# Reordering the first block of a convolution-and-MLP kernel: VectorE work pinned, halo from DRAM, plain output products, and last stores over three queues

## The chip, the cores and the metric

The kernel runs on one core of one Trainium2 chip. The metric is the time of one execution on the device, in microseconds (us). All timed runs told here were in the fast one of the two states in which executions of one program fall. Engine names in profile lines: PE is TensorE, PEld its weight loads, DVE VectorE, ACT ScalarE, POOL GpSimd, SP SyncE; a "q" after a name is the engine's own sequencer, where it issues DMAs. A record is one entry of the trace; each product of this kernel shows as two records.

## The reference

Each of 32,768 tokens has 192 channels. A causal convolution of seven taps, softmax-normalised per head, is followed by a two-layer MLP with silu:

```
w   = softmax(weight, axis=-1)                  # 8 heads, 7 taps
h   = causal_conv(x, w)                         # x: (8, 4096, 192); a sequence starts with 6 zeros
a   = h @ w_in                                  # 192 -> 2048
out = (a * sigmoid(a)) @ w_out                  # 2048 -> 192
```

## The kernel before

The tokens are worked off in 32 blocks of 1024. A block is turned by VectorE (transposes), convolved on VectorE (three channel groups of one first tap and six further taps; a half of the block also needs the six tokens before it, its halo), copied to both partition halves by DMA ("spread", tile `dup`), and multiplied on TensorE by `w_in` and `w_out` in four chunks j = 0..3. Blocks 1 to 31 use a form with fewer products and more additions. Block 0 has extra work, because all weights have to be rounded on VectorE first (`rounded`), with two steps of each rounding on ScalarE:

```
def rounded(dst, key):                     # cut: ten steps, here the order that matters
    nc.vector.tensor_single_scalar(ex, hi, ...)
    nc.vector.tensor_single_scalar(st, lo, ...)
    nc.vector.tensor_scalar(ex, ex, ...)
    nc.scalar.sign(st, st)                               # ScalarE
    nc.scalar.activation(ex, ex, AF.Copy, ...)           # ScalarE
    nc.vector.tensor_scalar(mh, hi, ...)
    ...                                                  # four scalar_tensor_tensor
def round_in(j):
    rounded(wr[j], ...)
    for e in range(2):
        nc.scalar.dma_start(out=ws[j][...], in_=wr[j][...])   # halves swapped
```

The first products of block 0 put each silu on ScalarE too, which frees a PSUM bank (the kernel has eight) for the next products:

```
def up_plain(b, j):
    hs = {...: bank() ...}
    for k, (a, n) in order:
        for e in range(2):
            nc.tensor.matmul(hs[a, n, e], rows(wr[j], e)[:, a, k, :], ...)
        if k == NK - 1:
            for e in range(2):
                nc.scalar.activation(g[:, n, e, :], hs[a, n, e], AF.Silu)
```

The opening, in program order (a scheduler may move what is not pinned with `pin`), and the stores:

```
for k in range(NK): turn_in(0, k)     # after the last: halo of the second half copied by DMA inside SBUF
round_in(0)
for k in range(NK): conv(0, k, 0..6); spread(0, k)      # cut
load(1); round_in(1)
for j in range(NJ): up_plain(0, j); round_in(j + 2) or round_out(...) and combine_out(...)
round_out, combine_out of the rest; then block 1's inputs, and block 0's down products in the fast form
...
nc.sync.dma_start(out=out_v[...], in_=osb[...])         # every store on SyncE's queue
```

## Time and profile before

| | before |
|---|---|
| time, median of 3 runs | 2504.85 us (2504.03 to 2505.95) |
| profiled span | 2502.0 us |
| TensorE busy | 2439.5 us, 98% of the span |
| first product of block 0 | 43.92 us |
| first product of block 1 | 138.52 us |
| last product to the end of the span | 2490.97 to 2502.0: 11.0 us |

How to read it: TensorE is all but full from block 1 on, and a block takes 75.9 us there (37.97 us for the products with `w_in`, called up, and 37.92 for those with `w_out`, called down).

### The profile page before, as it was taken

The numbers are of one execution on the slowest core, as the hardware profiler recorded it, in microseconds if no ns is written. First come the engines' busy times: TensorE is split into PE (matmuls) and PEld (weight loads), VectorE is DVE, ScalarE is ACT, GpSimd is POOL, SyncE is SP. The second block draws the span as 40 slices with busy tenths as digits, with TensorE's granted clock in tenths as the row PEclk, the third lists the DMA queues.
The fourth block names the chain that finished last, engine by engine and source line by source line (L and its number), as shares of the span: only waits on it lengthen the run. The fifth ranks groups of instructions, "written<-read, shape, count | busy, mean of one in ns | idle before, by whom it ended". The sixth has DMA issues, their size and how long they took to land.

```text
span 2502.0 us, 29772 instructions
## 1 busy us (share of the span) xinstructions
PE 2439.5 (98%) x11280; PEld 953.7 (38%) x11280; DVE 2056.0 (82%) x2758; ACT 980.1 (39%) x1763; POOL 71.4 (3%) x105
## 2 busy tenths in 40 slices
PE   1999999999999999999999999999999999999998
PEld 1434333443333443334443334433334433334332
DVE  7878888888889888889888888888898888898875
ACT  1344333443333443334443334433334433344432
POOL 4300000000000000000000000000000000000000
PEclk9999999999999999999999999999999999999999
DMA  6311222112222122222122221122221222221110
GB/s 135 75 36 34 51 49 41 38 34 43 51 43 47 30 40 46 51 43 41 36 35 51 51 40 38 34 43 51 43 47 30 43 43 51 42 42 35 35 39 13
DMA packets 451294, 110.78 MB, mean 44 GB/s; under 512 B 423952, under 2 KB 424848, under 8 KB 451152
## 3 DMA queue, kind: packets, MB, share of 16 engines
q1 hardware_dynamic: 447872, 101.00, 22.0%
q0 software_dynamic: 1664, 5.51, 0.8%
q10 hardware_dynamic: 1616, 2.39, 0.4%
q8 instruction: 88, 1.44, 0.3%
q14 instruction: 54, 0.44, 0.1%
HBM read 31.49 MB, written 25.17 MB: 23 GB/s over the span
## 4 chain that ended last, share of the span: by engine, by line
PE 97%; DVE 2%; DMA 1%; issue 0%; ACTq 0%; SPq 0%; POOL 0%; ACT 0%; DVEq 0%
PE ps L440 48%; PE ps L385 47%; PE ps L349 1%; DVE nat L299 1%; DMA raw<-in_moe_w_in_dram 0%; DVE two L183 0%; DMA dup<-nat 0%; DMA xt<-xt 0%; DVE mh L180 0%; DVE two L176 0%; ACTq L146 0%; DVE mh L171 0%; DVE two L164 0%; DVE two L165 0%; SPq L311 0%
## 5 line engine op out<-in xcount | busy, mean ns | idle before, releaser
L440 PE MATMUL ps<-g,wo 128*64 128x512 f32 x3072 | 901.4, 593 | 0.0
L385 PE MATMUL ps<-dup,ws 64*128 64x512 f32 x2480 | 869.9, 589 | 0.0
L409 DVE TENSOR_TENSOR g<-u,ps 128x512 f32<-128x512 f32 x744 | 488.5, 680 | 117.0 <-PE ps L385 103.2
L385 PE MATMUL ps<-win,wr 64*128 64x512 f32 x1488 | 567.7, 589 | 0.0
L440 PEld LDWEIGHTS ps<-g,wo 128*64 128x64 f32 x3072 | 284.5, 137 | 590.7 <-issue 567.2
L440 PE MATMUL ps<-t,wx 128*64 128x512 f32 x1024 | 481.2, 592 | 0.0
L406 ACT ACTIVATE g<-g 128x512 f32<-128x512 f32 x744 | 445.6, 631 | 88.1 <-DVE g L409 88.1
L385 PEld LDWEIGHTS ps<-dup,ws 64*128 64x128 f32 x2480 | 363.0, 187 | 292.0 <-issue 284.7
L499 ACT COPY cmb<-ps 64x512 f32<-64x512 f32 (+1 forms) x96 | 55.8, 581 | 997.5 <-PE ps L440 996.7
L299 DVE SCALAR_TENSOR_TENSOR nat<-xt,taps,nat 128x512 f32<-128x512 f32 x576 | 431.8, 750 | 11.1
L385 PE MATMUL ps<-dup,wr 64*128 64x512 f32 x992 | 419.9, 596 | 0.0
L440 PE MATMUL ps<-t,wo 128*64 128x512 f32 x1024 | 372.2, 592 | 0.0
L426 DVE TENSOR_TENSOR t<-g,t 128x1024 f32<-128x1024 f32 x256 | 313.4, 1224 | 68.0 <-PE ps L440 57.0
L400 ACT COPY u<-ps 128x512 f32<-128x512 f32 x496 | 277.8, 589 | 233.3 <-PE ps L385 233.3
L426 DVE TENSOR_TENSOR t<-g 128x1024 f32<-128x1024 f32 x256 | 308.9, 1218 | 0.0
L385 PEld LDWEIGHTS ps<-win,wr 64*128 64x128 f32 x1488 | 233.4, 187 | 175.3 <-issue 146.7
L385 PE MATMUL ps<-win,ws 64*128 64x512 f32 x496 | 242.2, 589 | 0.0
L440 PE MATMUL ps<-g,wx 128*64 128x512 f32 x512 | 240.6, 592 | 0.0
L385 PEld LDWEIGHTS ps<-dup,wr 64*128 64x128 f32 x992 | 160.5, 187 | 127.4 <-issue 120.1
L404 ACT ACTIVATE g<-ps 128x512 f32<-128x512 f32 x248 | 143.9, 596 | 79.9 <-PE ps L385 76.0
L400 DVE COPY u<-ps 128x512 f32<-128x512 f32 x248 | 166.3, 680 | 9.8 <-PE ps L385 5.9
L440 PEld LDWEIGHTS ps<-t,wx 128*64 128x64 f32 x1024 | 140.3, 137 | 0.0
(55 smaller groups left out, 974.5 us busy)
## 6 DMA issues: line engine op xcount, KB each, us to landing
dup<-nat SPq DMA_DIRECT2D x384, 128.0 KB, 2.3
nat<-in_x_dram SPq DMA_DIRECT2D x384, 64.0 KB, 2.4
out_dram<-osb SPq DMA_DIRECT2D x384, 64.0 KB, 1.9
raw<-in_moe_w_out_dram POOLq DMA_DIRECT2D x8, 384.0 KB, 4.6
raw<-in_moe_w_in_dram POOLq DMA_DIRECT2D x12, 192.0 KB, 5.1
ws<-wr ACTq DMA_DIRECT2D x8, 192.0 KB, 5.2
raw<-in_moe_w_in_dram ACTq DMA_DIRECT2D x4, 192.0 KB, 7.3
xt<-xt SPq DMA_DIRECT2D x32, 4.5 KB, 1.9
```

Of the source, the lines that this page charges most:

```text
L299: nc.vector.scalar_tensor_tensor(out=dst, in0=src, scalar=tap, in1=dst, op0=ALU.mult, op1=ALU.add)
L349: nc.tensor.matmul(hs[a, n, e], rows(wr[j], e)[:, a, k, :], rows(d, e)[:, n, k, :], start=k == 0, stop=k == NK - 1,)
L385: nc.tensor.matmul(bk[b, m, bn], rows(w, half), rows(v, half), start=first, stop=True, skip_group_check=True,)
L400: pin(copy(u, bk[b, m, "1"]))
L404: pin(nc.scalar.activation(g, bk[b, m, "1"], AF.Silu))
L406: pin(nc.scalar.activation(g, g, AF.Silu))
L409: pin(nc.vector.tensor_tensor(g, us.pop((b, m, i)), bk[b, m, bn], op=ALU.add))
L426: pin(nc.vector.tensor_tensor(t[i // 2][:, i % 2, :], u, v, op=ALU.subtract))
L440: nc.tensor.matmul(accs[b][i][R * half : R * half + R, :], lhs, rhs, start=first and j == 0, stop=j == NJ - 1, skip_group_check=True,)
L499: pin(nc.scalar.copy(*copies[name]()))
```

## The change

The intent is to start TensorE earlier. VectorE's work in the opening is kept in program order (`vec`), and that order is new: convolve the first channel group, round weight chunk 0, convolve the rest. The halo comes straight from DRAM, so that the first convolution need not wait for the third transpose. The loads are spread over two queues. Block 0's down products take a plain form without VectorE's sums. The last block's stores go out on three queues.

```
+    class Pinned: ...                       # every call of vec.X is pin(nc.vector.X(...))
+    vec = Pinned(nc.vector)
...
-                nc.sync.dma_start(
+                (nc.sync if b or k or i % 2 else nc.scalar).dma_start(
                     out=nat[...], in_=x_v[...]
...
+    xts[0] = xpool.tile(...)
+    nc.gpsimd.memset(xts[0][0:R, :, 0:pad], 0.0)
+    for k in range(NK):
+        nc.gpsimd.dma_start(out=xts[0][R:P, k, 0:pad], in_=x0[:, k, :], ...)
...
     load_in(0, nc.scalar)
-    load_in(1, nc.gpsimd)
+    load_in(1, nc.sync)
...                                          # rounding and softmax: nc.vector -> vec
+    def down_plain(b):                       # 96 products into three banks, then three copies on ScalarE
...
+            queue = (nc.sync, nc.scalar, nc.gpsimd)[q % 3] if b == NB - 1 else nc.sync
...
     for k in range(NK):
         turn_in(0, k)
-    round_in(0)
-    for k in range(NK):
         for i in range(K):
             conv(0, k, i)
         spread(0, k)
         if k == 0:
+            round_in(0)
             load_in(2, nc.gpsimd)
...                                          # combine_out moves behind the roundings and products
+    begin_down(0)
+    for _, s in zip_longest(down_plain(0), plan[NU:], fillvalue=()):
+        ...                                  # block 1's convolutions beside them
```

## The prediction

> **What bounds the kernel now.** I read the page's busy table first, then the chain that ended last in order of time for the first 140 us and for the end, then each engine's timeline over the same stretch.
>
> ```profile
> PE 2439.5 (98%) x11280; PEld 953.7 (38%) x11280; DVE 2056.0 (82%) x2758; ACT 980.1 (39%) x1763; POOL 71.4 (3%) x105
> PE 97%; DVE 2%; DMA 1%; issue 0%; ACTq 0%; SPq 0%; POOL 0%; ACT 0%; DVEq 0%
> ```
>
> TensorE bounds 31 of the 32 blocks, and the change leaves those alone. Only the opening and the tail can move. The chain there (start us, us, what):
>
> ```profile
> 59.41 0.67 DVE nat L299
> ...
> 61.88 4.30 DMA dup<-nat
> 66.18 0.04 issue
> 66.22 34.38 PE ps L349 x153
> 100.60 37.92 PE ps L440 x176
> 138.52 1.48 PE ps L385 x5
> ...
> 2453.03 37.94 PE ps L440 x176
> ...
> 2494.55 0.71 DVE osb L511
> ```
>
> Until 66.2 us the chain is DVE work and copies; from there PE runs without a break: up products of block 0, its down products, and block 1 at 138.5. The first block's timeline on PE (start, duration) shows what was done before 66.2:
>
> ```profile
> 43.92 6.17 PE L349 MATMUL ps<-dup,wr 64*128 64x512 f32 x16 [43.92 <-DMA dup<-nat]
> 55.45 5.65 PE L349 MATMUL ps<-dup,wr 64*128 64x512 f32 x16 [5.36 <-DMA dup<-nat]
> 62.33 3.08 PE L349 MATMUL ps<-dup,wr 64*128 64x512 f32 x6 [1.23 <-DMA dup<-nat]
> 66.22 34.38 PE L349 MATMUL ps<-dup,wr 64*128 64x512 f32 x154 [0.82 <-DMA dup<-nat]
> ```
>
> Steady rate: 37.92/176 = 0.2155 us a record. The 38 records done before 66.22 leave 10 of the first 48 (weight chunk j=0), so j=0 ended near 68.4. The rest of block 0 took 138.5 - 68.4 = 70.1.
>
> The pieces whose durations I reuse, from the DVE and ACT timelines:
>
> ```profile
> 86.97 4.76 DVE L299 SCALAR_TENSOR_TENSOR nat<-xt,taps,nat 128x512 f32<-128x512 f32 x6
> 25.96 1.09 DVE L186 SCALAR_TENSOR_TENSOR wr<-mh,two 128x768 f32<-128x768 f32 x1
> 22.36 0.84 ACT L169 ACTIVATE two<-two 128x768 int32<-128x768 int32 x1 [6.18 <-DVE two L165]
> 78.62 4.97 ACT L359 ACTIVATE g<-ps 128x512 f32<-128x512 f32 x10
> 41.09 21.39 SPq L311 DMA_DIRECT2D dup<-nat  x12
> 2486.35 13.09 SPq L517 DMA_DIRECT2D out_dram<-osb  x12
> ```
>
> A convolution of one channel group is a transpose 0.65, a first tap 0.62 and six taps 4.76: 6.0 us. A rounding of one weight chunk ran from 21.34 to 27.05: 5.7 us, of which ACT gives a sign and a copy, 0.8 each. A silu of a bank takes 0.50. Copies to both halves (dup) landed 4.2 us after the first of four issues (41.09 to 45.29).
>
> **What the Trainium skill says.** "TensorE: Matmul & The Clock Gate", architectural detail: ScalarE and VectorE are strict FIFO queues. The trace has nothing against it, and it decides my number. Same page, Part 1 (the HAM clock gate): matmuls after an idle spell run at half clock for about 3.4 us. The trace agrees roughly: the first 16 records took 6.17 us, against 16 x 0.2155 = 3.45. "DMA: Bandwidth & Descriptors", "Issuing engines are not separate DMA queues": more queues save only issue time. Before, one x load or store takes 0.3 to 0.5 us to issue, so that time is all I credit. Same page, "Rules for kernel authors": a non-contiguous last dimension becomes one descriptor per element; the halo load is such a one (3 x 384 elements of 4 bytes). No run yet shows its cost.
>
> **The change part by part.**
>
> *(a) Start of the convolution.* Before, the first tap waited at 32.41 for the halo copied out of the third transpose. After, the halo comes from DRAM early. The built order on DVE is: softmax of the taps, convolution k=0, rounding 0, k=1, k=2, roundings 1, 2, 3, then the four of w_out, then block 1. The exponential now stands on ACT behind four weight loads, three of which wait for earlier loads to free a completion semaphore. The first x loads landed at 4.75 and 5.18 before; I estimate the last weight issue at 6.2, the table load (1.28) and exponential at 7.9, and seven small DVE groups (1.9) at 9.8. So the transpose starts at T0 = 10. I estimate the halo landing near 8: hidden.
>
> *(b) First products.* k=0 convolved 16.0; rounding 0 ends 21.7; products of k=0 start at 21.8 and, cold, take 6. k=1 convolved 27.7, landed 31.9, products 5.7 more. k=2 convolved 33.7, landed 38.0, products 3.4: j=0 ends at 41.5. Against 68.4 that is 26.9 us earlier.
>
> *(c) Plain down products.* Fast form 176 records, plain form 4 x 2 x 2 x 3 x 2 = 96 products = 192 records: 16 more x 0.2155 = +3.4 us. The sixteen sums on DVE (1.22 each, some 19 us) go away, but PE did not wait for them.
>
> *(d) ACT.* If PE stayed fed from 41.5, block 1 would begin at 41.5 + 70.1 + 3.4 = 115, a gain of 23.5. I don't expect that. Before, DVE was four roundings further when PE ran dry of waits; now six lie behind. In the built order ACT must do, in this sequence: eight silus of j=0; sign and copy of rounding 2; silus 1-2 of j=1; rounding 3; silus 3-4; silu 5, sign of the first w_out rounding, silu 6, its copy; silus 7-8; second w_out rounding; silus 1-2 of j=2; third; silus 3-4; fourth; and only then silus 5-8 of j=2. A sign waits for DVE, DVE for a weight load, and that load for its buffer. Strict order makes these waits hold the silus, silus hold PSUM banks, and banks hold PE.
>
> Step by step: rounding 1 ends 39.5. The sign of rounding 2 follows the last j=0 silu (43.1), so rounding 2 ends 47.8. Its successor's load stands on POOL behind combinations that wait for j=0's products: issued at 44.2, and 768 KB took 6.5 us at 28.46 to 34.97, so rounding 3 runs 50.7 to 56.3. First w_out rounding 56.3 to 62.5. Second, load issued 56.5 once a buffer is free: 62.7 to 68.2. Third, load behind further combinations, issued 65.2, landed 71.4: ends 77. Fourth: ands 77 to 77.9, sign and copy to 79.5. Silus 5-6 of j=2 end 80.5; the third of four product groups of j=3 (2.57 each) can then start, and the fourth follows: 80.5 + 5.2 = 85.7. Without waits it would be 41.5 + 31 = 72.4. So 13.3 us are lost.
>
> Block 1 then begins at 85.7 + 192 x 0.2155 = 127.1, against 138.5: gain 11.4. DVE's roundings end 82.6; with transposes (2), halo copy (4), three convolutions (16), copies (4) and window differences (3) block 1's inputs are ready near 112: hidden.
>
> *(e) Tail.* The last transpose ended at 2495.9, and the last eight of the twelve stores went out one after another from 2495.3 to 2499.4, the last landing at 2500.9. With SP taking half, ACT and POOL a quarter each, SP's fourth goes out at about 2497.3 and lands 1.9 later: 1.6 to 1.8 gained if POOL's two land by then.
>
> Sum: 2504.85 - 11.4 - 1.8 = 2491.7; I say 2491.5.
>
> **Rivals.**
> 1. *Nothing blocks*: gain 23.5 + 1.8, time 2479.5. For it: PE had no wait after 66.2 before, with roundings interleaved in ACT's stream too. Against it: those signs came while DVE was ahead; now it is behind. Even six roundings at 5.7 us with no load wait put the last copy near 70 us, when its silus should serve a group at 67.
> 2. *More blocking*: x loads of block 1 and weight loads collide from 38 us on (before, a load took 6.8 us in such a stretch), or DVE slows beside POOL (taps took 0.86 instead of 0.66 us at 45 us). Three to six us more on the rounding chain: 2495 to 2498.
> 3. *The halo load is slow*: if 1152 single elements land at 15 instead of 8, T0 shifts 5 us, all of it felt: 2496.
> 4. *The tail's POOL stores are slow* and become the last: gain of the tail 0 instead of 1.8: 2493.5.
>
> **Range and chances.** Rival 1 gives the low end, 2 and 3 the high end; the waits of (d) are a robust order but each load is uncertain by 1 to 2 us. 8 in 10: 2481 to 2498. A 2% gain is 50 us, and the opening has only about 58 us before effective full speed, so: faster 0.01, within 2% 0.98, slower 0.01.
>
> **What would show it.** First tap near 11 us without a wait on a copy; j=0's last product near 41; PE idle in j=2 and j=3 of the first block, waits put down to silus, about 13 us in all; ACT idle there until DVE's roundings; block 1's first product near 127; stores from three queues ending near 2.3 us after the first. It is wrong if PE is busy from 41 to 115 (rival 1), if the first tap waits for the halo load, or if block 1's products wait for DVE.

## The result and the profile after

The changed kernel took 2495.45 us (median of 4 fast runs, 2495.21 to 2496.86), the kernel before in the same rounds 2504.44 us (2503.96 to 2505.95): 9.0 us less. Ratios here are the mean time of one kernel's fast runs over that of the other's of the same rounds, so not quite the ratio of the medians quoted: 0.9964, 95% interval 0.9947 to 0.9982. That is within 2%, and inside the range predicted.

The changed kernel's page, busy times and the chain that ended last (shares of the span by engine):

```profile
PE 2450.4 (98%) x11296; PEld 956.8 (38%) x11296; DVE 2038.6 (82%) x2736; ACT 976.7 (39%) x1759; POOL 74.1 (3%) x107
PE 96%; DVE 3%; ACT 0%; DMA 0%; issue 0%; ACTq 0%; POOL 0%; POOLq 0%; DVEq 0%
```

DVE's share of the chain has grown from 2 to 3%. The same chain in order of time (start, us, what) says where:

```profile
81.56 0.84 ACT two L186
83.68 5.90 PE ps L367 x23
89.58 41.35 PE ps L497 x192
```

Before, the chain was on TensorE from 66.2 us. Now it runs over VectorE's roundings (tiles `two`, `mh`, `wr`, `wo`) and a sign on ScalarE (line L186) until 83.68, and only then over TensorE's last up products (L367) and the plain down products (L497). TensorE's timeline of block 0 (start, duration, engine, line, what, count, and in brackets the idle time before and what ended it):

```profile
21.38 6.61 PE L367 MATMUL ps<-dup,wr 64*128 64x512 f32 x16 [21.38 <-DVE wr L109]
29.43 10.93 PE L367 MATMUL ps<-dup,wr 64*128 64x512 f32 x32 [1.45 <-DMA dup<-nat]
43.03 24.24 PE L367 MATMUL ps<-dup,wr 64*128 64x512 f32 x96 [2.67 <-ACT g L377]
69.58 3.33 PE L367 MATMUL ps<-dup,wr 64*128 64x512 f32 x12 [2.31 <-ACT g L377]
76.64 5.67 PE L367 MATMUL ps<-dup,wr 64*128 64x512 f32 x12 [3.73 <-ACT g L377]
83.68 5.90 PE L367 MATMUL ps<-dup,wr 64*128 64x512 f32 x24 [1.37 <-ACT g L377]
89.51 41.42 PE L497 MATMUL ps<-g,wo 128*64 128x512 f32 x192
```

Chunk j=0 is done at 29.43 + 10.93 = 40.4, against about 68.4 before: 28 us won. Then TensorE waits four times for a silu (L377), 2.67 + 2.31 + 3.73 + 1.37 = 10.1 us. There is a second loss in the same lines. The 144 records from 43.03 on would take 31.0 us at the steady 0.2155 us each. They end at 89.58, 49.2 us after 40.4, so 49.2 - 31.0 - 10.1 = 8.1 us were lost in records that ran slowly. The clock that the trace grants TensorE changes only in steps of 3.41 us here, so windows are cut at these steps. Behind the stretch stand the busy times of the engines PE, PEld, DVE, ACT, POOL; the third number from the end is the clock granted to TensorE, as a share of full speed. The third line is from another kernel with the same opening (the half stores below):

```profile
44.33:47.74 3.41, 3.41 (x10) 1.81 (x8) 0.58 (x1) 3.41 (x8) 0.00 (x0) 0.50 1.11 181
75.05:81.87 6.82, 5.23 (x12) 3.62 (x12) 6.75 (x9) 2.33 (x5) 4.67 (x6) 0.50 0.19 73
```

```profile
84.93:88.34 3.41, 3.41 (x10) 1.78 (x8) 3.38 (x5) 2.56 (x6) 1.50 (x4) 0.50 0.00 0
```

By an estimate from the first two lines, half the clock cost 1.7 us in the first stretch and 2.6 us in the second (TensorE was busy for 5.23 us of it), 4.3 of the 8.1 us. About 1.1 us more was lost at 59.91 to 61.86, where four records started in 1.95 us instead of 0.86 while ScalarE gave silus one at a time. The rest, some 2.7 us, fits the four restarts: even at a clock of 1.00, the 24 records from 83.68 took 5.83 us until the down products began at 89.51, instead of 5.17, since after a wait the second bank came free 0.49 us after the first.

Whether a wait costs clock depended on how it fell on the steps. In this trace the steps in which TensorE idled for 1.45 to 2.14 us were followed by one at 0.50, those with 0.95 to 1.37 us were not. (In the kernel of the third line 1.50 us was followed by one and 1.62 us was not, so this is no threshold.) The steps lie differently in each execution: in that kernel one more fell on the last 24 records, which took 7.60 instead of 5.90 us, and block 1 began at 132.45 instead of 130.86.

Why TensorE waits is on ScalarE's timeline:

```profile
41.08 1.28 ACT L377 ACT_TABLE_LOAD   x1 [4.77 <-DVE two L109]
42.38 4.03 ACT L377 ACTIVATE g<-ps 128x512 f32<-128x512 f32 x8
81.56 0.84 ACT L186 ACTIVATE two<-two 128x768 int32<-128x768 int32 x1 [4.49 <-DVE two L109]
83.05 4.97 ACT L377 ACTIVATE g<-ps 128x512 f32<-128x512 f32 x10
```

At 81.56 ScalarE had been idle for 4.49 us. It stood at the sign of the last rounding, whose input VectorE had just made. Behind it in the queue stood ten silus, and by 82.31 all eight banks were full (168 of the 192 records were done, six to a bank, and only 20 silus). The ten ran one after another from 83.05. At 41.08 it shows the same for the first silus. They had stood behind two copies of swapped weights (`ws<-wr`, issued from 39.91, once the second rounding was done) and then had to load the silu table.

### The profile page after: what moved, and what is told of

Its sections match the earlier page's. It is cut to its first block, busy times and chain, and to the rows that moved or that the text cites. A ratio compares the mean times of both kernels' runs of the same rounds, so it can differ in the third digit from the quotient of the medians.

```text
span 2493.8 us, 29780 instructions
## 1 busy us (share of the span) xinstructions
PE 2450.4 (98%) x11296; PEld 956.8 (38%) x11296; DVE 2038.6 (82%) x2736; ACT 976.7 (39%) x1759; POOL 74.1 (3%) x107
## 4 chain that ended last, share of the span: by engine, by line
PE 96%; DVE 3%; ACT 0%; DMA 0%; issue 0%; ACTq 0%; POOL 0%; POOLq 0%; DVEq 0%
PE ps L403 47%; PE ps L458 47%; PE ps L497 2%; DVE two L109 1%; DVE nat L317 0%; DVE mh L109 0%; DMA nat<-in_x_dram 0%; PE ps L367 0%; ACT g L377 0%; DVE wr L109 0%; DVE xt L297 0%; DVE wo L109 0%; ACT two L186 0%; DVE nat L314 0%; DVE u L544 0%
## 5 line engine op out<-in xcount | busy, mean ns | idle before, releaser
L458 PE MATMUL ps<-g,wo 128*64 128x512 f32 x2976 | 873.2, 593 | 0.0
L458 PEld LDWEIGHTS ps<-g,wo 128*64 128x64 f32 x2976 | 275.6, 137 | 572.2 <-issue 548.7
L458 PE MATMUL ps<-t,wx 128*64 128x512 f32 x992 | 466.1, 592 | 0.0
L317 DVE SCALAR_TENSOR_TENSOR nat<-xt,taps,nat 128x512 f32<-128x512 f32 x576 | 431.4, 749 | 11.9
L458 PE MATMUL ps<-t,wo 128*64 128x512 f32 x992 | 360.5, 592 | 0.0
L444 DVE TENSOR_TENSOR t<-g,t 128x1024 f32<-128x1024 f32 x248 | 303.6, 1224 | 60.7 <-PE ps L458 50.2
L444 DVE TENSOR_TENSOR t<-g 128x1024 f32<-128x1024 f32 x248 | 299.3, 1218 | 0.0
L458 PE MATMUL ps<-g,wx 128*64 128x512 f32 x496 | 233.1, 592 | 0.0
L418 DVE COPY u<-ps 128x512 f32<-128x512 f32 x248 | 166.3, 680 | 11.9 <-PE ps L403 8.3
L422 ACT ACTIVATE g<-ps 128x512 f32<-128x512 f32 x248 | 143.9, 596 | 79.5 <-PE ps L403 75.6
L553 DVE STREAM_TRANSPOSE osb<-cmb 128x512 f32<-128x512 f32 x96 | 67.5, 704 | 101.9 <-ACT cmb L541 79.0
```

Of the source, the lines that this page charges most:

```text
L317: nc.vector.scalar_tensor_tensor(out=dst, in0=src, scalar=tap, in1=dst, op0=ALU.mult, op1=ALU.add)
L418: pin(copy(u, bk[b, m, "1"]))
L422: pin(nc.scalar.activation(g, bk[b, m, "1"], AF.Silu))
L444: pin(nc.vector.tensor_tensor(t[i // 2][:, i % 2, :], u, v, op=ALU.subtract))
L458: nc.tensor.matmul(accs[b][i][R * half : R * half + R, :], lhs, rhs, start=first and j == 0, stop=j == NJ - 1, skip_group_check=True,)
L553: nc.vector.transpose(osb[:, i, :, :].rearrange("p k c -> p (k c)"), cmbs[b][0][:, i, :])
```

## The experiments

Eight kernels were aimed at the reasons; then came a better version, and three more that change one part of it each. Each was run with the kernel before on the same chip; that one's medians were 2504.57, 2504.19 and 2503.77 in the three groups, so a difference of less than about 1 us between groups is not read from times alone.

**Is it ScalarE's order?** Theory: the sign and copy of a rounding stand ahead of silus whose banks are full. Rivals: VectorE's roundings themselves, or TensorE's down products. The first kernel changes no work at all, it only keeps ScalarE's silus and rounding steps in program order:

```
-        nc.scalar.sign(st, st)
-        nc.scalar.activation(ex, ex, AF.Copy, ...)
+        pin(nc.scalar.sign(st, st))
+        pin(nc.scalar.activation(ex, ex, AF.Copy, ...))
...
-                    nc.scalar.activation(g[:, n, e, :], hs[a, n, e], AF.Silu)
+                    pin(nc.scalar.activation(g[:, n, e, :], hs[a, n, e], AF.Silu))
```

> The changed kernel with ScalarE pinned to program order: all eight silus of one weight chunk stand ahead of the sign and copy of the next rounding. Same work, only the order on ScalarE differs. Theory (strict order on ScalarE puts VectorE's roundings ahead of the silus, full PSUM banks then hold TensorE): TensorE's three waits for silus of 2.3, 3.7 and 1.4 us go, the plain down products start near 74 instead of 89.5, block 1 near 116 to 118 instead of 130.9, the time falls by 12 to 15 us to about 2482. Rival (TensorE waits in the end for the weight chunks, or block 1 for VectorE, whatever ScalarE's order): within 2 us of 2495.5, with waits moved to the rounded weights.

Measured: 2483.51 us (2483.13 to 2484.07), ratio 0.9915 [0.9902, 0.9929], correct. That is 11.9 us under the changed kernel, a little less than the 12 to 15 expected. TensorE's timeline:

```profile
43.05 33.35 PE L367 MATMUL ps<-dup,wr 64*128 64x512 f32 x144 [2.68 <-ACT g L377]
76.33 41.42 PE L497 MATMUL ps<-g,wo 128*64 128x512 f32 x192
```

All 144 records in one stretch: three of the four waits are gone, and with them most of the slow records (33.35 for 144, 2.3 above the steady rate). The wait before 43.03 stays, since it comes from the weight copies and the table load. So the order on ScalarE carries the loss, as theory had it. VectorE now waits instead: four times for a sign, 3.11 to 4.95 us each. The last sign starts at 90.01 instead of 81.56, so the roundings are later than before, and TensorE does not wait for them.

The second kernel takes sign and copy away from ScalarE altogether and gives them to VectorE:

```
-        nc.scalar.sign(st, st)
-        nc.scalar.activation(ex, ex, AF.Copy, bias=-float(896 * 8 * one), scale=8.0)
+        vec.tensor_single_scalar(st, st, 1, op=ALU.min)
+        vec.tensor_scalar(ex, ex, scalar1=-float(896 * one), scalar2=8.0, op0=ALU.add, op1=ALU.mult)
```

> The changed kernel with the sign and the scaling of each rounding done by VectorE (two more instructions of about 0.5 us for each of eight roundings, some 8 us of VectorE work more) and none of it on ScalarE. Theory: although VectorE has more to do, no silu waits for a rounding and no rounding for a silu: block 1 starts near 115, the time falls by about 15 us to 2480. Rival (VectorE's own work is what holds TensorE): the time rises by up to 8 us, to 2500 to 2503.

Measured: 2487.46 us (2486.77 to 2488.15), ratio 0.9931 [0.9917, 0.9945], correct: better than the changed kernel by 8.0 us, but some 7 us short of what was expected. ScalarE's timeline holds a reason for part of that:

```profile
58.37 1.12 ACTq L213 DMA_DIRECT2D ws<-wr  x2
```

This issue of the swapped weights of the last `w_in` chunk waits until its rounding is done, and ScalarE's silus stand behind it: eight ran in one go from 59.53, and TensorE waited 3.51 us until 60.18. Here the issue of a DMA from ScalarE's queue held the silus just as a sign did; the expectation had overlooked it.

**Does GpSimd slow the roundings?** In the changed kernel the roundings between 51.4 and 80.3 us took 7.1 to 7.4 us each (the second took 6.6, the last 6.4), where the prediction had used 5.5 to 6.2. They lie beside GpSimd's combinations of weights. This kernel leaves those out, so it computes a WRONG result (relative error 1.49):

```
 def comb(out, u, v, op):
-    nc.gpsimd.tensor_tensor(out, u, v, op=op)
+    return                     # and wx filled with zeros once
```

> The changed kernel with GpSimd's 44 combinations of weights left out and the tiles that they fill zeroed early (a wrong result on purpose; all the rest is the same work). From 51 us on a rounding took 7.1 to 7.4 us, where the first took 5.7. Theory (GpSimd's combinations slow VectorE): roundings of 5.7 us again, the last sign near 75.5 instead of 82, block 1 near 123 to 124, about 7 us less: 2488. Rival (DMA traffic of the weight loads, or the instructions' own cost): the roundings stay at 7 us and the time within 2 us of 2495.5.

Measured: 2489.23 us (2488.57 to 2490.56), ratio 0.994 [0.9925, 0.9955]. Two VectorE instructions of the last rounding, first in the changed kernel, then without the combinations:

```profile
74.41 0.81 DVE L109 TENSOR_SCALAR two<-two 128x768 int32<-128x768 int32 x1
75.88 1.20 DVE L109 SCALAR_TENSOR_TENSOR two<-raw,two 128x768 int32<-128x768 int32 x1
```

```profile
68.85 0.54 DVE L109 TENSOR_SCALAR two<-two 128x768 int32<-128x768 int32 x1
69.84 0.96 DVE L109 SCALAR_TENSOR_TENSOR two<-raw,two 128x768 int32<-128x768 int32 x1
```

The same instructions are a quarter to a half longer beside GpSimd. Without it a rounding takes about 5.9 us, the last sign starts at 74.63 instead of 81.56, and block 1 at 123.9 instead of 130.9. So GpSimd's work, which is on no chain, costs the changed kernel about 6 us. It does so by way of the silus that wait for the roundings: with ScalarE in program order (above) the roundings end at 95.4 instead of 86.7 us and TensorE has no such wait. (Leaving the combinations out was not tried there.)

**What is the tail worth?** First all stores of the last block on SyncE again:

```
-            queue = (nc.sync, nc.scalar, nc.gpsimd)[q % 3] if b == NB - 1 else nc.sync
+            queue = nc.sync
```

> The changed kernel with the last block's stores all on the SP queue, as before. By the prediction three queues are worth 1.8 us, so this would be 2497.3; by the trace of the changed kernel the time from the last product to the end fell from 11.0 to 10.2 us only, so 0.8 us: 2496.3. From the trace: eight stores issued within 2 us land 3.3 to 4.0 us after issue instead of 1.9, so it is the transfer and not its issue that ends last.

Measured: 2495.97 us (2495.74 to 2497.61, 5 runs), ratio 0.9967 [0.9954, 0.9979], correct. The median is 0.5 us above the changed kernel's, which the intervals do not separate. From the last product to the end of the span it is 10.8 us here, 10.3 in the changed kernel and 11.0 before, so 0.5 to 0.7 us. The prediction had 1.8 us. (The expectation misreads one thing: of the last eight stores only the last four landed 3.3 to 4.0 us after issue, the first four 2.0 to 3.0.) Why so little came of it is a matter of the landings, so the next kernel stores only half of each chunk of the last block, with the same number of issues (WRONG, half of the last block's rows stay unwritten):

```
+            h = 8 if b == NB - 1 else 16
             queue.dma_start(
-                out=out_v[...][:, :, c : c + SQ], in_=osb[..., i, :, :]
+                out=out_v[...][:, 0:h, c : c + SQ], in_=osb[..., i, 0:h, :]
```

> WRONG on purpose: the changed kernel, whose last block stores only the first half of each of its twelve chunks, so half the descriptors and bytes from the same three queues with the same issues; half of the last block's rows are not written. It measures whether the tail is bound by the transfer of the stores. In the changed kernel the last eight stores were issued within 2 us and landed 3.3 to 4.0 us after issue, and the time from the last product to the end was 10.2 us. Theory (transfer-bound: 128-byte pieces saturate the engines): landing falls to 2.0 to 2.5 us and the tail to 8.7 to 9.2 us, time about 1.2 us less, 2494.3. Rival (a fixed completion time and issue cost bind it): landing stays above 3 us, tail 9.9 to 10.2, 2495.4.

Measured: 2495.66 us (2495.39 to 2495.92), ratio 0.9966 [0.9951, 0.9981]. The time alone would have decided for the rival. But the profiled execution had the opening with the slow last 24 records (block 1 at 132.45, 1.6 us later than in the profile of the changed kernel); what opening the other three runs had is not known. Counted from the last product, the tail was 9.0 us, 1.3 less than with whole stores. The DMA issues of the end (queue, count, KB each, median us from issue to landing), SyncE's line for one queue, for three queues, for three queues with half stores (its window takes in two earlier stores), and for three queues in the best version below:

```profile
out_dram<-osb SPq DMA_DIRECT2D x8, 64.0 KB, 1.9
```

```profile
out_dram<-osb SPq DMA_DIRECT2D x4, 64.0 KB, 2.9
```

```profile
out_dram<-osb SPq DMA_DIRECT2D x6, 32.0 KB, 1.7
```

```profile
out_dram<-osb SPq DMA_DIRECT2D x4, 64.0 KB, 3.4
```

With three queues the issues take 2 instead of 4 us, but each store then lands later, because the transfers pile up (186 GB/s at the most in the 1-us windows, against 128 from one queue). With half the bytes landing is fast again. So here the end is bound by the transfer of these small stores as much as by their issue. What three queues are worth is not settled: the seven kernels of this document that have them and whole stores, up to the best version, show tails of 10.2 to 10.5 us, but the best version and its three variants 11.3 to 11.5, no better than one queue. Why their stores land later is not known.

**Undo one part at a time.** Three kernels undo one part of the change each. The halo as before, that is by a copy after the third transpose, with the order of work that this needs:

```
-    x0 = ...; for k in range(NK): nc.gpsimd.dma_start(out=xts[0][R:P, k, 0:pad], in_=x0[:, k, :], ...)
...
-            if b:
+            if True:
                 nc.sync.dma_start(out=xt[R:P, :, 0:pad], in_=xt[0:R, :, TB : TB + pad])
...
 for k in range(NK):
     turn_in(0, k)
+round_in(0); load_in(2, nc.gpsimd)
+for k in range(NK):
     conv(0, k, 0..6); spread(0, k)
```

> The changed kernel with the first block's halo copied inside SBUF as before (all three transposes, then the copy, rounding 0 beside it, then the three convolutions, all pinned). The prediction's part (a) says that the early halo load lets the first convolution start at 10. Here the transposes end near 14.4 (the last x load landed at 13.7), rounding 0 ends near 20 and covers the copy, the three convolutions end near 36 and rounding 1 near 43, 3 us later than in the changed kernel; since VectorE's roundings carry the chain from there, the time rises by about 3 us to 2498.5. Rival (the halo load is no gain, roundings have slack): within 1 us of 2495.5.

Measured: 2498.64 us (2496.95 to 2500.19, two runs near 2497 and two near 2500), ratio 0.9977 [0.9962, 0.9992], correct. The number is the expected one, the mechanism is not: the last rounding ended at 85.2, even before the changed kernel's 86.7, and j=0 at 42.1. TensorE's last wait:

```profile
81.00 13.54 PE L362 MATMUL ps<-dup,wr 64*128 64x512 f32 x46 [2.96 <-ACT g L372]
```

Here 46 records instead of 24 follow the last wait: the scheduler had placed ScalarE's unpinned silus differently, with more of them behind the last signs. So this run does not tell what the halo itself is worth.

Block 0's down products in the fast form:

```
-    begin_down(0)
-    for _, s in zip_longest(down_plain(0), plan[NU:], fillvalue=()): ...
+    ...                                                             # combine_out moves back before it
+    run(0, [[t for t in s if t[0] in "tiv"] for s in plan[:NU]])    # with VectorE's sums (t)
+    for b in range(NB): ...                                         # the general loop, as before
```

> The changed kernel with block 0's down products in the fast form again (176 records instead of 192, and sixteen sums of 1.22 us on VectorE among block 1's convolutions). The prediction's part (c) says that TensorE did not wait for the sums, so the plain form costs 3.4 us: then this is 2492. Theory now: in the changed kernel VectorE is free of roundings only at 86.6, so the sums come late, TensorE waits for them, and block 1 starts near 133 instead of 130.9: 2497 to 2500, the plain form being worth 2 to 5 us.

Measured: 2500.05 us (2499.29 to 2500.53), ratio 0.9983 [0.9968, 0.9998], correct: 4.6 us above the changed kernel, with 16 records fewer. TensorE waits inside the down products for a sum:

```profile
98.97 0.61 PE L458 MATMUL ps<-t,wx 128*64 128x512 f32 x1 [4.58 <-DVE t L444]
```

VectorE's program order not kept in roundings and softmax:

```
-    vec = Pinned(nc.vector)
+    vec = nc.vector
```

> The changed kernel without the pins on VectorE's roundings and softmax. The built order then puts two roundings between the taps of the first block's second and third convolution and one wait for weights into the softmax: first products later by some 10 us, but roundings 1 and 2 done earlier. Theory (the chain runs over roundings, signs and silus, and silus of the third chunk now stand behind the last sign): the plain early gain is lost or turned, 2497 to 2500. Rival (early convolution is what counts): 10 us worse, 2505.

Measured: 2501.23 us (2500.7 to 2502.0), ratio 0.9987 [0.997, 1.0004], correct: 5.8 us above the changed kernel, a little over the range expected. The scheduler put roundings ahead of convolutions: the products of the second channel group began at 37.18 instead of 29.43. Then the same wait as in the changed kernel, longer:

```profile
78.76 4.76 PE L367 MATMUL ps<-dup,wr 64*128 64x512 f32 x12 [6.76 <-ACT g L377]
```

**A version that beats both.** The order on ScalarE kept as in the first experiment, the swapped weights copied from SyncE's queue, and the silu table loaded early by a silu of one column right after the exponential:

```
+    warm = const.tile([P, 1], F32, name="warm")
+    nc.scalar.activation(warm, wexp[:, 0, 0:1], AF.Silu)
...
-            nc.scalar.dma_start(out=ws[j]...
+            nc.sync.dma_start(out=ws[j]...
```

> The kernel with ScalarE in program order, plus the half-swapping copies of w_in issued on SP instead of ScalarE and the silu table loaded at the start by a one-column silu. Theory (in the pinned kernel the first silu still waited for two such copies and the table, 42.4 instead of 38): TensorE has no wait of 2.7 us at 43, roundings 2 and 3 end 3 us sooner, block 1 starts near 113.5 to 115 instead of 117.7: 2479 to 2481. Rival (block 1 now waits for VectorE's last convolution, which moves less): within 1.5 us of 2483.5.

Measured: 2480.33 us (2480.20 to 2480.51), ratio 0.9904 [0.9889, 0.9919], correct. That is 15.1 us under the changed kernel. TensorE's timeline:

```profile
36.51 35.70 PE L369 MATMUL ps<-dup,wr 64*128 64x512 f32 x160 [0.70 <-DMA dup<-nat]
72.13 41.42 PE L499 MATMUL ps<-g,wo 128*64 128x512 f32 x192
113.48 1.55 PE L405 MATMUL ps<-dup,wr 64*128 64x512 f32 x5
```

No wait from 36.51 to block 1. VectorE's last window difference for block 1 ended at 113.77, and the first product that reads one began at 114.45: VectorE has hardly any slack left here. Block 1 begins 17.4 us earlier than in the changed kernel, and 2 us of that come back. Block 1's up products take 39.1 instead of 37.97 us: the halo copy of block 2 stands behind twelve stores on SyncE's queue, VectorE waits 2.21 us for it until 130.35, and TensorE 0.68 us at 133.50. And the tail is 11.3 instead of 10.3 us. How much the copies' queue and the table are worth each was not tried apart; together they gained 3.2 us.

**The parts again, with ScalarE's order out of the way.** The three last kernels change one part each of this best version.

The halo by a copy (edit as in the earlier halo run):

> The halo of the first block comes from the third transpose again, in the version with ScalarE's order kept, the copies of the swapped weights on SyncE and the silu table loaded early (2480.33). With ScalarE's order fixed only VectorE's order of convolutions moves. Worked out from rows of that version: transposes at 10.4 to 12.5, rounding 0 until 18.2, the three convolutions (5.2 us each without the transpose) until 33.8, so rounding 1 starts at the same time as there (33.9), but the products of the first channel group start near 27.5 instead of 22.06 and, cold, the 48 records of j=0 end near 41 instead of 39.9. Theory (the early halo by itself is worth little, because the copy hides behind rounding 0): about 1 us slower, 2481.5, 2480.5 to 2482.5. Rival (the early halo is worth several us, as in the run that undid it alone): 2483.5 or more, with waits of TensorE beyond the first products.

Measured: 2481.27 us (2481.10 to 2481.45), ratio 0.9909 [0.9894, 0.9924], correct; 0.9 us more, too little to be read from times of two groups alone, but block 1 began 1.28 us later (114.76). As expected, TensorE starts later but then without a break:

```profile
28.21 45.27 PE L364 MATMUL ps<-dup,wr 64*128 64x512 f32 x192 [28.21 <-DMA dup<-nat]
```

It ends at 73.5, 1.3 us after the best version, although its first product came 6.15 us later. The last product of j=0 ended at 42.33 instead of 41.36 (the 39.9 of the expectation was too early): an earlier first product is worth only about what that last one gains.

The loads on the queues as before:

```
-                (nc.sync if b or k or i % 2 else nc.scalar).dma_start(
+                nc.sync.dma_start(
...
-    load_in(1, nc.sync)
+    load_in(1, nc.gpsimd)
```

> The first loads as before the change: all twelve x loads on SyncE's queue, the second weight chunk's on GpSimd's, in the same version (2480.33). Theory (the opening is paced by VectorE from the first transpose on, and that stood at 10.39): the first group's last x load is issued behind others and the exponential's place on ScalarE moves earlier, so the transpose starts between 10 and 13; time 2480 to 2483.5, moving by as much as the first transpose does. Rival (the loads' queues matter for nothing): 2480.3 with the first transpose at 10.4; or, if weights on GpSimd's queue come late, a wait before the second rounding.

Measured: 2482.31 us (2482.11 to 2482.95), ratio 0.9913 [0.9899, 0.9928], correct; 2.0 us more. VectorE's first transpose waits for the x load:

```profile
13.00 0.71 DVE L299 STREAM_TRANSPOSE xt<-nat 128x512 f32<-128x512 f32 x1 [4.19 <-DMA nat<-in_x_dram]
```

It starts 2.61 us later than the 10.39 of the best version, and block 1's first product 2.73 us later (116.21). The opening is paced by VectorE from its first transpose on.

The fast form of block 0's down products (edit as above):

> The first block's down products in the fast form (16 records fewer, 3.4 us; 16 sums of 1.2 us on VectorE) in the same version (2480.33). There VectorE's last window ended at 113.8, just as block 1's products began at 113.48: it has no slack left. Theory (what the plain form buys is VectorE time): the 19.5 us of sums now stand on the path, the down products wait for them and block 1's inputs come later; block 1 begins 10 to 20 us later than 113.5, total 2490 to 2500. Rival (TensorE's 3.4 us count, sums are hidden): 2477.

Measured: 2504.41 us (2504.25 to 2505.37), ratio 1.0001 [0.9984, 1.0018], correct. The direction was expected, not the size: 24.1 us more than the best version, all of the gain over the kernel before.

```profile
102.69 1.09 PE L460 MATMUL ps<-t,wx 128*64 128x512 f32 x1 [26.22 <-DVE t L446]
```

TensorE did 18 records of the down products and then waited 26.22 us for the first sum that they need. VectorE finished the roundings at about 91, then turned the next block, waited 2.06 us for its halo, convolved, and only came to the sums at 100.07. Block 1 began at 139.47, where it had been in the kernel before.

All results together (where block 1 begins is read on TensorE's timeline; the 138.52 above is from the chain, where the same product follows the one before it):

| kernel | median us | block 1 begins | against the changed kernel |
|---|---|---|---|
| before | 2504.44 | 138.45 | +9.0 |
| changed | 2495.45 | 130.86 | |
| ScalarE in program order | 2483.51 | 117.68 | -11.9 |
| sign and copy on VectorE | 2487.46 | 122.5 | -8.0 |
| no combinations (wrong) | 2489.23 | 123.9 | -6.2 |
| last stores on one queue | 2495.97 | 132.30 | +0.5 |
| last stores halved (wrong) | 2495.66 | 132.45 | +0.2 |
| halo copied | 2498.64 | 135.8 | +3.2 |
| fast down form | 2500.05 | 135.12 | +4.6 |
| VectorE not pinned | 2501.23 | 137.2 | +5.8 |
| best | 2480.33 | 113.48 | -15.1 |
| best, halo copied | 2481.27 | 114.76 | -14.2 |
| best, loads as before | 2482.31 | 116.21 | -13.1 |
| best, fast down form | 2504.41 | 139.47 | +9.0 |

The single losses do not add up: undoing halo, down form and pinning one by one costs 3.2, 4.6 and 5.8 us, together more than the whole gain of 9.0. The parts depend on one another.

## Why the prediction was right or wrong

The time (2491.5 predicted, 2495.45 measured) lay in the range, and the mechanism that decided it was the predicted one. Step by step:

*(a) Start of the convolution: right.* The first transpose started at 9.72 (predicted 10), the first tap at 10.46 without a wait for the halo, whose three loads landed at 6.22, 7.80 and 8.99. (The trace counts 96 packets for their 1152 elements; descriptors it does not count.) That the new queues of the loads help was not given a number; on the best version they were worth 2.0 us.

*(b) First products: right.* j=0 ended at 40.4 (predicted 41.5). The first 16 records took 6.61 us (predicted 6). That makes some 5 us at half clock rather than the 3.4 cited, an estimate from the 2.5 us lost beside the restart; the trace's clock record begins only at 27.26 and does not show this stretch.

*(c) Plain down products: the size was right, the reason for it wrong.* 192 records took 41.35 us, 3.4 more than 176 take. But the prediction booked this as a cost, since TensorE "did not wait for them", the sums. That held in the kernel before. With TensorE's up products done 11 us earlier (changed kernel) or 28 us earlier (best version) it no longer holds: the fast form costs 4.6 us in the changed kernel and 24.1 in the best one. The plain form is what makes room on VectorE.

*(d) ScalarE: the mechanism was right, the term was too small.* "Strict order makes these waits hold the silus, silus hold PSUM banks, and banks hold PE" is what the waits show, and keeping the order on ScalarE, with no work changed, gained 11.9 us. The term "So 13.3 us are lost" measured 18.2 us (10.1 of waits and 8.1 of slow records). Three things made it larger. The first silus started at 42.38, not near 39.2, behind the weight copies and the table load. Four roundings took 7.1 to 7.4 us where 5.5 to 6.2 were booked. The prediction named a slower VectorE beside GpSimd in its rival 2 and did not put it into the sum; leaving the combinations out gave back 6.2 us, and the measured time lies in the 2495 to 2498 that rival 2 gave. And records after a wait were booked at the full rate, though the prediction cited the slow clock after idling and used it in step (b); low clock is 4.3 of the 8.1 us. In the other direction, one link of the chain did not occur: no rounding of the opening waited for a weight load. The prediction had booked such waits (47.8 to 50.7 and 68.2 to 71.4), but the load of chunk 3 was issued at 39.19, not at 44.2, and had landed at 49.8, before VectorE was free. So it is partly luck that the end of ScalarE's last copy (predicted 79.5, measured 83.1) came out so near. Block 1 began at 130.9 where 127.1 was predicted.

*(e) Tail: too large.* 1.8 us were booked for the saved issues; 0.5 (times) to 0.7 (profile) were measured in the changed kernel and nothing in the best version, since the stores of three queues landed 2.0 to 4.0 us after issue instead of 1.7 to 1.9.

The sum was thus 11.4 + 1.8 = 13.2 booked, and 9.0 measured: 3.8 of the difference from (d) with the small credit of (b), about 1 from (e). (The terms come from one profile each and fit the times to within about 1 us.) Of the rivals, "nothing blocks" (2479.5) did not happen, but the best version, which takes the blocks away, lands within 1 us of it. "The halo load is slow" and the late stores of GpSimd did not happen.

Two points stay open: why the last stores land later in the best version and its variants than in the other kernels with three queues, and what the early halo is worth in the changed kernel itself, where the run that undid it also moved ScalarE's silus. On the best version it is worth about 1 us.

## What to carry to other kernels

When one engine is brought forward by tens of microseconds, look at every in-order queue that feeds it and ask what stands ahead of what it needs: here two short ScalarE steps and a DMA issue, each waiting for VectorE, held full PSUM banks, and pinning them in program order was worth more than the whole change. A form that trades products on the busiest engine against sums on another is only cheap while that other engine has slack; measure it again after each reordering. A part's worth is best measured on a version in which the larger wait is already gone.

## What the Trainium skill lacked or had wrong

- "TensorE: Matmul & The Clock Gate", section "HAM oscillation — how this bites in real kernels", gives the rule "no PE-idle gaps >~3.4µs". Here TensorE was granted half the clock after shorter gaps: 1.45 us of idling (27.98 to 29.43) was followed by 0.50 from 30.68 to 34.09, and 2.67 us by 0.50 from 44.33 to 47.74. Gaps of 2.31 and 1.37 us were not followed by a lower clock.
- "SBUF — State Buffer", section "Who interferes with whom", says that VectorE instructions with two SBUF inputs contend with GpSimd instructions that read SBUF. The runs agree (such an instruction went from 0.96 to 1.20 us), but the page has no size for mixed work: whole roundings went from about 5.9 to 7.1-7.4 us. An instruction with one input went from 0.54 to 0.81 us; whether that was one of the two-port modes, for which the page says the same, no run shows.
- No page gives the cost of a small load made of single elements: three loads of 384 elements of 4 bytes each took 0.66 to 0.80 us of GpSimd's time to issue and landed 4.8 to 6.1 us after it, which was hidden here. How much of that is due to the elements and how much to the loads beside it is not shown.
